# Agent attention with a squared-ReLU layer: the first batch's keys, weight parts, query transposes and table transfers in another order

## The chip, the cores and the metric

One core of a Trainium2 chip runs the kernel. The metric is the device time of one execution in microseconds (us). The kernel before took 2059.75 us, the median of three runs (2058.2 to 2061.1).

## What is computed

Two layers of attention through 49 agents, in four batches of 12480 tokens of width 128, and then a layer with a squared ReLU (128 to 2048 to 128), all in float32:

```python
def _attn_ref(q, k, v, agents):
    scale = 1.0 / np.sqrt(q.shape[-1])
    def sm(a, b):
        s = scale * (a @ b.transpose(0, 2, 1))
        s = s - s.max(-1, keepdims=True)
        e = np.exp(s)
        return e / (e.sum(-1, keepdims=True) + 1e-09)
    a2k = sm(agents, k)
    agent_v = a2k @ v
    q2a = sm(q, agents)
    return (q2a @ agent_v).astype(np.float32)

def _moe_ref(x, w_in, w_out):
    h = np.maximum(x @ w_in, 0.0)
    return (h * h @ w_out).astype(np.float32)
```

`w_in` and `w_out` come as 64-bit floats, and the kernel makes its 32-bit parts of them itself.

## The kernel before, in words

**The main loop.** The product of `agent_v` and `w_in` is made once for each batch: a table of 49 rows and 2048 columns, kept as a rounded part `aw_hi` (rows 0 to 97, with 30 rows of the rest below them) and the last 19 rows of the rest, `aw_ex`, in four places of 32 partitions (`tables`, L323). The queries of a group of 960 tokens become weights over the agents (`queries`, L354): scores (L362), softmax, a split into halves, two transposes (L384), and for each half group j a tile `w` with 30 rows copied below its 98 (L392) and a tile `x` with 19 rows copied to four places (L394). One step k of the main loop then takes two of the 16 column chunks of `w_in` for 480 tokens. `first(k)` (L404) multiplies table and weights for k and k+1 into two PSUM tiles `h` of two banks each; `hidden` (L422) makes `r` (ReLU) and `g_hi` on ACT, and `gg` and `g_lo` on DVE (on POOL for even k); `second(k)` (L447) comes four steps later and sums twelve products with `wo_hi` and `wo_lo` into `o`. 416 pairs of steps are 52 groups in four batches.

**The work beside it.** While a batch runs, `background` (L464) makes the next batch's table: scores of 13 key blocks (`scores`, L181), maxima, exponentials and values. Its steps are dealt out by `goal` (L592).

**The first batch.** Nothing runs beside it, so lines 497 to 579 do the same with other helpers and in an order written out by hand: `queued` (L56) chains the instructions of each engine in the order in which the code issues them (`alone[0]` true). Twelve key blocks of 512 KB, and a small one, are loaded into ten buffers `ahead` by SP, with parts of the weights (`raw`, 256 KB, five buffers) between them (L517 to L528). A block's scores are eight matmuls of 98 columns into both banks of one `h`, a maximum `mx` on DVE and a copy `s` on ACT. Between the blocks stand the decodes of weight parts: ACT takes an absolute value (`begun`, L126), DVE five instructions (`decoded`, L131), POOL a sum (`make_w_in`, L147), or, for a part of `w_out`, ACT a cast `wo_hi` and POOL two instructions (`make_w_out`, L151). Six parts of `w_in` are made among the keys.

Then follow the maxima over all keys (`maxima`, L210) and the values loop (L547): for each block DVE subtracts the maximum (`s<-s,mb`), ACT takes the exponential, PE multiplies with the values, and POOL adds up the exponentials in `mx`. Seven more weight parts are made between them, and the first group's queries go through their steps (`q0`, L563). `whole_sums` (L268) closes the batch, `tables(0)` makes the table: four matmuls `h<-win,avT`, four `aw_hi` on ACT, four `aw_lo` on DVE, and the transfers of L346 to L349, a first set of five for the first 512 columns and a second set of five for the rest. Two of the first set's four `aw_ex` transfers are issued by ACT (L348). The first loads for the second batch and for the second group's queries are asked for just ahead of the table (L572 to L576); the last three weight parts are made in the main loop (L610).

A DMA runs on the queue of the engine that issues it, nearly always SP, and SP takes its instructions in order: one that waits for a buffer or for its source holds all behind it.

Of the kernel before, what the change touches and what calls it, by code (L numbers as in the profile page):

```python
# [17 lines left out]
P = 128  # L18
TP = 120
NT = 8  # L20
# [9 lines left out]
WARM = 16  # L30
PRE = 10
RAW = 5
LATE = 3
SPREAD = 0.88


# [1 line left out]
def agent_attention_relu2(ctx: ExitStack, tc: tile.TileContext, qT, kT, v, agT, w_in, w_out, outT):  # L38
# [142 lines left out]
    def scores(b, i, kt):  # L181
        st = state.setdefault(b, {"s": []})
        _, rows, nt = blocks[i]
        if alone[0]:
            h = ps_h.tile([P, 2, 512], F32, name="h")[:rows, :, :].rearrange("p h (t x) -> p h t x", x=P)
            n = nt // 2
            for t in range(nt):
                out = h[:, t // n, t % n, : 2 * NA]
                keys = kt[:, t * rows : (t + 1) * rows]
                pe.matmul(out, keys, ag[:, :2, :].rearrange("c b a -> c (b a)"), start=True, stop=True)  # L190
            sv = h[:, :, :n, :NA]
        else:
            sv = bank()[:rows, : nt * NA].rearrange("p (t a) -> p t a", a=NA)
            for t in range(nt):
                pe.matmul(sv[:, t, :], kt[:, t * rows : (t + 1) * rows], ag[:, b, :], start=True, stop=True)  # L195
        yield
        s = sp.tile([P, NT, NA], F32, name="s")
        st["s"].append(s)
        if i == 0:
            st["mx"] = small.tile([P, NT, NA], F32, name="mx")  # L200
        s, mx = (x[:rows, :nt, :] for x in (s, st["mx"]))
        if alone[0]:
            s, mx = (x.rearrange("p (h t) a -> p h t a", h=2) for x in (s, mx))
        if i == 0:
            dve.tensor_copy(mx, sv)
        else:
            dve.tensor_max(mx, mx, sv)
        act.copy(s, sv)
# [58 lines left out]

    def whole_sums(b):  # L268
        st = state[b]
        e1 = small.tile([P, 2, NA], F32, name="e1")  # L270
# [52 lines left out]
    def tables(b):  # L323
# [6 lines left out]
        for n in range(FF // 512):  # L330
# [14 lines left out]
            cs = slice(ns.start * 512, ns.stop * 512)  # L345
            sync.dma_start(hi[K2:, cs].bitcast(F32), lo[:SP, cs].bitcast(F32))  # L346
            for t in range(NQ):
                by = act if alone[0] and n == 0 and t % 2 else sync  # L348
                by.dma_start(ex[t * 32 : t * 32 + NL, ns, :].bitcast(F32), apart[SP:, ns, t, :].bitcast(F32))  # L349


    weights = {}
# [140 lines left out]
    def run(gen):  # L493
        for _ in gen:
            pass
# [8 lines left out]
    with tc.tile_pool(name="pre", bufs=PRE) as pre, tc.tile_pool(name="dec", bufs=2) as dec:  # L504
# [8 lines left out]
        def next_values():  # L513
            vts.append(load_values(0, len(vts), pre, "ahead"))

        between = {i: n for n, i in enumerate((3, 4, 6, 7, 9, 10))}
        for i in range(NK):  # L517
            kts.append(load_keys(0, i, pre, "ahead"))
            if 1 <= i <= NW:
                raws[i - 1] = ask_w_in(dec, i - 1)  # L520
            if i == NK - 3:
                q0 = queries(0)
                next(q0)
# [4 lines left out]
                make_w_in(between[i], part)  # L528
        for n in range(10):
            next_values()  # L530
            if n < 3:
                raws[NW + n] = ask_w_out(dec, n)
        top = maxima(0)
        next(top)
# [1 line left out]
        next(top)  # L536
        warm(3)
        next(top)
        warm(6)
        run(top)  # L540
        for i in range(3):
            whole_exps(0, i, dve)
        for i in range(2):
            add_weights(0, i)
        between = {i: n + 6 for n, i in enumerate((0, 2, 3, 5, 7, 8, 10))}
        part = begun(dec, raws.pop(6))
        for i in range(NK):  # L547
            if i + 3 < NK:
                whole_exps(0, i + 3, dve)
# [3 lines left out]
            if i in between:  # L553
# [2 lines left out]
                    make_w_in(n, part)  # L556
                else:
                    make_w_out(n - NW, part)
                if n < NW:
                    raws[n + 5] = ask_w_out(dec, n + 5 - NW)  # L560
                if n + 1 in raws:
                    part = begun(dec, raws.pop(n + 1))
            if i not in (6, 7, 8, 9):  # L563
                next(q0, None)
            if len(vts) < NK:
                next_values()
            if i == NK - 2:
                ends = whole_sums(0)
                next(ends)
        run(q0)  # L570
        run(ends)
        raws = [ask_w_out(late, NW - LATE + n) for n in range(LATE)]  # L572
        todo = background(1)
        next(todo)
        ahead = queries(1)
        next(ahead)  # L576
        run(tables(0))
        next(ahead)
        next(ahead)
    behind = [chain[eng] for eng in (nc.sync, nc.scalar, nc.vector, nc.gpsimd)]  # L580

    alone[0] = False
    ffn = ctx.enter_context(tc.tile_pool(name="ffn", bufs=4))
# [1 line left out]
    for k in range(total + LAG):  # L585
        if k < total:
            g, c = divmod(k, SLOTS)
            b, i = divmod(g, NB)
            if i == 0 and c == 0 and 0 < b < B - 1:
                todo = background(b + 1)  # L590
                done = 0
            goal = (i * SLOTS + c + 1) * STEPS / (SPREAD * NB * SLOTS)  # L592
            while done < goal and step(todo):
                done += 1
            if c == 0 and 0 < g < B * NB - 1:
# [4 lines left out]
        if k % 2 == 0:  # L600
# [6 lines left out]
            copied_out()  # L607
            if hs:
                hidden(k + 1, hs[1])
            if raws:  # L610
                alone[0] = True
                make_w_out(NW - len(raws), begun(late, raws.pop(0)))
                alone[0] = False


# [33 lines left out]
```

## Time and profile before

| | |
|---|---|
| median of three runs | 2059.75 us |
| the profiled execution | 2060.47 us |
| its span | 2058.7 us |
| PE busy | 2022.0 us (98%) |
| ACT busy | 1769.0 us (86%) |
| DVE busy | 1683.2 us (82%) |
| POOL busy | 1271.2 us (62%) |
| mean granted clock of PE | 0.987 |

The profile's busy times are shares of the whole span. The change touches only the first 150 us or so, so the views to read are those by time: the timeline of each engine there, and busy time in stretches of 10 us. In a timeline a row has the start, the length, the engine, the line, the operation with output and inputs, and in brackets the idle time ahead of it with what ended it. Matmuls in float32 show as two or more records each.

### The profile page before, as it was taken

Reading aid. Unit: us, or ns where it says so; the run is one execution under the profiler, and the core shown is the slowest. Engines: PE = TensorE matmul, PEld = TensorE weight load, DVE = VectorE, ACT = ScalarE, POOL = GpSimd, SP = SyncE. Lnnn points to the kernel's source line nnn. Section 1 sums busy time; section 2 is a strip of 40 time slices with the busy share of each in tenths; the row PEclk is TensorE's granted clock in tenths of the full one; section 3 lists DMA queues with packets and bytes.
Section 4 is the critical chain, followed back from the end, with each engine's and each line's share of the span. In section 5 each row is a group of like instructions: output and inputs, shape, how many; then the busy total and the mean of one; then the engine's idle time right before and its main releaser. Section 6 shows DMA issues by size and latency. Waiting matters only on the chain. (4 is left out here: it accounts for less than half of the span.)

```text
span 2058.7 us, 31652 instructions
## 1 busy us (share of the span) xinstructions
PE 2022.0 (98%) x10950; PEld 1592.8 (77%) x10950; DVE 1683.2 (82%) x1843; ACT 1769.0 (86%) x2100; POOL 1271.2 (62%) x1103
## 2 busy tenths in 40 slices
PE   8799999999999999999999999999999999999999
PEld 8578777777788777777778877777777777777777
DVE  5577888888877888888887788888888888888887
ACT  2277999998977899999987799998889999999998
POOL 2354777865644577776554468776555565656565
PEclk9689999999999999999999999999999999999999
DMA  8322121211122121212112212221111111111100
GB/s 323 106 88 92 50 79 59 72 59 57 43 75 80 59 65 57 81 52 75 44 56 71 76 38 64 75 63 43 38 53 37 46 37 42 36 47 35 39 23 20
DMA packets 55552, 131.35 MB, mean 64 GB/s; under 512 B 6560, under 2 KB 35184, under 8 KB 55392
## 3 DMA queue, kind: packets, MB, share of 16 engines
q1 hardware_dynamic: 55352, 129.31, 19.5%
q8 instruction: 87, 1.43, 0.3%
q14 instruction: 73, 0.60, 0.1%
q10 hardware_dynamic: 40, 0.02, 0.0%
HBM read 80.97 MB, written 25.56 MB: 52 GB/s over the span
## 5 line engine op out<-in xcount | busy, mean ns | idle before, releaser
L435 POOL TENSOR_TENSOR g_lo<-gg,g_hi 128x480 fp32r<-128x480 f32 x832 | 999.8, 1223 | 681.2 <-DVE gg L59 424.0
L59 ACT ACTIVATE r<-h 128x960 f32<-128x960 f32 x832 | 802.0, 964 | 165.8 <-PE h L59 154.4
L59 ACT ACTIVATE g_hi<-r 128x960 fp32r<-128x960 f32 x832 | 838.1, 1007 | 32.3 <-POOL e L234 0.4
L59 DVE TENSOR_TENSOR h<-r,h 128x960 f32<-128x960 f32 x416 | 482.2, 1159 | 165.1 <-ACT r L59 160.9
L59 DVE TENSOR_TENSOR gg<-r,h 128x960 f32<-128x960 f32 x416 | 477.5, 1148 | 82.3 <-ACT r L59 78.9
L59 PE MATMUL o<-g_hi,wo_hi 128*128 128x480 f32 x1664 | 538.2, 404 | 0.0
L59 DVE TENSOR_TENSOR g_lo<-h,g_hi 128x960 fp32r<-128x960 f32 x416 | 480.8, 1156 | 47.4 <-ACT g_hi L59 10.6
L59 PE MATMUL h<-w,aw_hi 128*128 128x480 f32 x1664 | 487.9, 398 | 7.5 <-DVE gg L59 6.8
L59 PE MATMUL o<-g_hi,wo_lo 128*128 128x480 f32 x1664 | 494.4, 378 | 0.0
L59 PE MATMUL o<-g_lo,wo_hi 128*128 128x480 f32 x1664 | 494.3, 378 | 0.0
L59 PEld LDWEIGHTS o<-g_hi,wo_hi 128*128 128x128 f32 x1664 | 280.4, 188 | 117.2 <-issue 67.8
L59 PEld LDWEIGHTS o<-g_hi,wo_lo 128*128 128x128 f32 x1664 | 312.5, 188 | 47.3
L59 PEld LDWEIGHTS o<-g_lo,wo_hi 128*128 128x128 f32 x1664 | 312.5, 188 | 47.0
L59 PEld LDWEIGHTS h<-w,aw_hi 128*128 128x128 f32 x1664 | 289.3, 190 | 53.7 <-DVE gg L59 18.8
L59 PE MATMUL h<-x,aw_ex 19*128 19x480 f32 x1664 | 204.7, 481 | 0.6 <-DMA x<-w 0.6
L59 PEld LDWEIGHTS h<-x,aw_ex 19*128 19x128 f32 x1664 | 80.1, 182 | 141.1 <-issue 139.5
L362 PEld LDWEIGHTS psa<-ag,qt 128*120 128x120 f32 x800 | 99.5, 184 | 6.9 <-issue 0.7
L59 DVE COPY ob<-o 128x480 f32<-128x480 f32 x104 | 68.2, 655 | 34.7 <-PE o L59 33.8
L362 PE MATMUL psa<-ag,qt 128*120 128x49 f32 x800 | 94.6, 260 | 0.0
L195 PEld LDWEIGHTS psa<-ag,kt 128*128 128x128 f32 (+1 forms) x588 | 78.9, 202 | 14.3 <-DMA kt<-in_kT 8.5
L234 POOL TENSOR_TENSOR vs<-vt,vs 128x1024 fp32r<-128x1024 f32 (+1 forms) x39 | 81.6, 2094 | 11.2 <-ACT vs L232 10.6
L195 PE MATMUL psa<-ag,kt 128*128 128x49 f32 (+1 forms) x588 | 76.4, 280 | 9.3 <-DMA kt<-in_kT 7.7
(113 smaller groups left out, 1022.7 us busy)
## 6 DMA issues: line engine op xcount, KB each, us to landing
qt<-in_qT SPq DMA_DIRECT2D x52, 480.0 KB
out_T<-ob SPq DMA_DIRECT2D x104, 240.0 KB
kt<-in_kT SPq DMA_DIRECT2D x36, 512.0 KB
vt<-in_v SPq DMA_DIRECT2D x36, 512.0 KB
x<-w SPq DMA_DIRECT2D x416, 35.6 KB
ahead<-in_kT SPq DMA_DIRECT2D x12, 512.0 KB
ahead<-in_v SPq DMA_DIRECT2D x12, 512.0 KB
w<-w SPq DMA_DIRECT2D x104, 56.2 KB
```

Of the source, the lines that this page charges most:

```text
L59: ins = issue(*args, **kw)
L195: pe.matmul(sv[:, t, :], kt[:, t * rows : (t + 1) * rows], ag[:, b, :], start=True, stop=True)
L234: eng.tensor_sub(out[:, :, n : n + w], x, out[:, :, :w].bitcast(F32))
L362: pe.matmul(sv[:, t, :], qt[:, t * TP : (t + 1) * TP], ag[:, b, :], start=True, stop=True)
L435: nc.gpsimd.tensor_sub(lo[:, n, :], gg[:, n, :], hi[:, n, :].bitcast(F32))
```

## The change

Nine edits, all in the first batch's part of the program or at the start of the main loop:

1. **Key blocks.** Two blocks share one `h`, one bank each, eight matmuls one behind the other in a bank; before, each block took a tile of two banks.
2. **Weight parts in the key loop.** The sixth to eighth part of `w_in` are asked for behind key blocks 7, 8 and 9 where it was 6, 7 and 8, and seven parts are made there, after blocks 3, 4, 5, 7, 8, 10 and 11, where it was six.
3. **Weight parts in the values loop.** Five are made (the last of `w_in`, four of `w_out`) where it was seven. Four, not three, have buffers of their own (`LATE`), and all four are asked for in the values loop. One of them is made right behind the table, three in the main loop.
4. **The next loads.** The second group's queries and the second batch's first key block are asked for at step 3 of the values loop; before, ahead of the table.
5. **Query transposes.** The steps of `q0` skip the values loop's steps 5 to 7 and no longer run on behind it, so that the two transposes stand behind the ninth and the eleventh block.
6. **Sums.** `whole_sums` begins at the third last block, not the second last, and uses a buffer `d`.
7. **Table transfers.** SP issues all of them.
8. **Main loop.** No background step is dealt out in the first four steps k; `goal` catches up at the fifth.
9. **Ties.** Background steps are also ordered behind PE's last instruction of the first part. Two more warming matmuls stand in the maxima.

```diff
-            h = ps_h.tile([P, 2, 512], F32, name="h")[:rows, :, :].rearrange("p h (t x) -> p h t x", x=P)
...
+            if i % 2 == 0:
+                st["h"] = ps_h.tile([P, 2, 512], F32, name="h")
+            h = st["h"][:, i % 2, :]
...
-                by = act if alone[0] and n == 0 and t % 2 else sync
-                by.dma_start(ex[t * 32 : t * 32 + NL, ns, :].bitcast(F32), apart[SP:, ns, t, :].bitcast(F32))
+                sync.dma_start(ex[t * 32 : t * 32 + NL, ns, :].bitcast(F32), apart[SP:, ns, t, :].bitcast(F32))
...
-        between = {i: n for n, i in enumerate((3, 4, 6, 7, 9, 10))}
+        asked = {i: n for n, i in enumerate((1, 2, 3, 4, 5, 7, 8, 9))}
+        between = {i: n for n, i in enumerate((3, 4, 5, 7, 8, 10, 11))}
...
-            if 1 <= i <= NW:
-                raws[i - 1] = ask_w_in(dec, i - 1)
+            if i in asked:
+                raws[asked[i]] = ask_w_in(dec, asked[i])
...
-        between = {i: n + 6 for n, i in enumerate((0, 2, 3, 5, 7, 8, 10))}
-        part = begun(dec, raws.pop(6))
+        between = {i: n + 7 for n, i in enumerate((0, 2, 4, 6, 8))}
+        part = begun(dec, raws.pop(7))
...
-            if i not in (6, 7, 8, 9):
-                next(q0, None)
             if len(vts) < NK:
                 next_values()
-            if i == NK - 2:
+            if i == 3:
+                held = [ask_w_out(late, NW - LATE + n) for n in range(LATE)]
+                ahead = queries(1)
+                next(ahead)
+                todo = background(1)
+                next(todo)
+            if i not in (5, 6, 7):
+                next(q0, None)
+            if i == NK - 3:
                 ends = whole_sums(0)
                 next(ends)
-        run(q0)
         run(ends)
-        raws = [ask_w_out(late, NW - LATE + n) for n in range(LATE)]
-        todo = background(1)
-        next(todo)
-        ahead = queries(1)
-        next(ahead)
         run(tables(0))
         next(ahead)
         next(ahead)
-    behind = [chain[eng] for eng in (nc.sync, nc.scalar, nc.vector, nc.gpsimd)]
+        make_w_out(NW - len(held), begun(late, held.pop(0)))
+    behind = [chain[eng] for eng in (nc.tensor, nc.sync, nc.scalar, nc.vector, nc.gpsimd)]
...
-            goal = (i * SLOTS + c + 1) * STEPS / (SPREAD * NB * SLOTS)
+            goal = (i * SLOTS + c + 1) * STEPS / (SPREAD * NB * SLOTS) if k >= 4 else 0
```

SP's queue from the last value load to the table's second set, before (`w_587` and `x_588` are the first half group's query weights, `w_692` and `x_693` the second's; `raw` are weight parts, `qt` and `kt` the next queries and keys):

```order
L59 DMA ahead<-in_v 96x256
L59 DMA w_587<-w_587 30x480
L59 DMA x_588<-w_587 19x480 x4
L59 DMA w_692<-w_692 30x480
L59 DMA x_693<-w_692 19x480 x4
L59 DMA raw<-in_w_out 128x2x256 x3
L59 DMA kt<-in_kT 128x1024
L59 DMA qt<-in_qT 128x960
L59 DMA aw_hi<-aw_lo 30x512
L59 DMA aw_ex<-aw_lo 19x128 x2
L59 DMA aw_hi<-aw_lo 30x1536
L59 DMA aw_ex<-aw_lo 19x3x128 x4
```

and in the change, with the numbers 646 and 679 for the two half groups:

```order
L59 DMA ahead<-in_v 96x256
L59 DMA raw<-in_w_out 128x2x256 x4
L59 DMA qt<-in_qT 128x960
L59 DMA kt<-in_kT 128x1024
L59 DMA w_646<-w_646 30x480
L59 DMA x_647<-w_646 19x480 x4
L59 DMA w_679<-w_679 30x480
L59 DMA x_680<-w_679 19x480 x4
L59 DMA aw_hi<-aw_lo 30x512
L59 DMA aw_ex<-aw_lo 19x128 x4
L59 DMA aw_hi<-aw_lo 30x1536
L59 DMA aw_ex<-aw_lo 19x3x128 x4
```

The five big loads have moved ahead of both sets of query weights, and both of these sets, ten transfers, now stand right ahead of the table's.

ACT at the end of the values loop, before (`pp` is the split of the query weights, `t` the start of a decode, `s` an exponential, `w_587` and `w_692` the copies of the two transposes):

```order
L59 CAST w_587<-h 98x480
L59 ACTIVATE s<-s 128x392 x2
L59 CAST wo_hi<-t 128x256
L59 ACTIVATE t<-raw 128x256
L59 ACTIVATE s<-s 128x392
L59 CAST wo_hi<-t 128x256
L59 ACTIVATE t<-raw 128x256
L59 ACTIVATE s<-s 96x98
L59 CAST wo_hi<-t 128x256
L59 CAST w_692<-h 98x480
L59 COPY avT<-h 128x49
L59 ACTIVATE aw_hi<-h,rl 98x512
```

and in the change:

```order
L59 CAST wo_hi<-t 128x256
L59 ACTIVATE t<-raw 128x256
L59 ACTIVATE s<-s 128x392 x2
L59 CAST wo_hi<-t 128x256
L59 CAST w_646<-h 98x480
L59 ACTIVATE s<-s 96x98
L59 CAST w_679<-h 98x480
L59 COPY avT<-h 128x49
L59 ACTIVATE aw_hi<-h,rl 98x512 x4
```

The first copy of a transpose has moved from behind the second `wo_hi` to behind the fourth and last one, so the two copies stand one exponential apart.

PE from the values to the first `first`, before (`psa<-ag,kt` are key scores of the second batch, `h<-ag,qt` scores of the second group, `h<-s,ahead` the values):

```order
L59 MATMUL h<-s,ahead 128x98 x48
L59 MATMUL h<-identr,pp 98x120 x4
L59 MATMUL h<-s,ahead 128x98 x48
L59 MATMUL h<-identr,pp 98x120 x4
L59 MATMUL h<-s,ahead 128x98 x2
L59 MATMUL h<-ones,e_695 98x1
L59 MATMUL h<-win,avT 98x512 x4
L195 MATMUL psa<-ag,kt 128x49 x8
L59 MATMUL h<-ag,qt 120x49 x8
L59 MATMUL h<-w_587,aw_hi 128x480 x4
L59 MATMUL h<-x_588,aw_ex 128x480 x4
```

and in the change:

```order
L59 MATMUL h<-s,ahead 128x98 x72
L59 MATMUL h<-identr,pp 98x120 x4
L59 MATMUL h<-s,ahead 128x98 x16
L59 MATMUL h<-identr,pp 98x120 x4
L59 MATMUL h<-s,ahead 128x98 x10
L59 MATMUL h<-ones,d 98x1
L59 MATMUL h<-win,avT 98x512 x4
L59 MATMUL h<-ag,qt 120x49 x8
L193 MATMUL psa<-ag,kt 128x49 x5
L59 MATMUL h<-w_646,aw_hi 128x480 x2
L193 MATMUL psa<-ag,kt 128x49 x3
L59 MATMUL h<-w_646,aw_hi 128x480 x2
```

The transposes stand three blocks later, and the key scores no longer stand ahead of the queries. Up to `second(0)` PE now has the scores of two key blocks and no transposes of the second group, where it had three key blocks and both transposes. From about the hundredth row on, in the second group of queries, the orders of all five engines are the same in both kernels.

More of the change, by code (lines that the diff above doesn't have):

```diff
@@ L32 @@
 RAW = 5
-LATE = 3
+LATE = 4
 SPREAD = 0.88
@@ L184, in scores @@
         if alone[0]:
-            h = ps_h.tile([P, 2, 512], F32, name="h")[:rows, :, :].rearrange("p h (t x) -> p h t x", x=P)
[L186 to L191, printed above, removed]
-        else:
-            sv = bank()[:rows, : nt * NA].rearrange("p (t a) -> p t a", a=NA)
-            for t in range(nt):
-                pe.matmul(sv[:, t, :], kt[:, t * rows : (t + 1) * rows], ag[:, b, :], start=True, stop=True)
+            if i % 2 == 0:
+                st["h"] = ps_h.tile([P, 2, 512], F32, name="h")
+            h = st["h"][:, i % 2, :]
+            agents, wide = ag[:, :2, :].rearrange("c b a -> c (b a)"), 2 * NA
+        else:
+            h, agents, wide = bank(), ag[:, b, :], NA
+        for t in range(nt):
+            out = h[:rows, t * NA : t * NA + wide]
+            pe.matmul(out, kt[:, t * rows : (t + 1) * rows], agents, start=True, stop=True)
+        sv = h[:rows, : nt * NA].rearrange("p (t a) -> p t a", a=NA)
         yield
@@ L201, in scores @@
         s, mx = (x[:rows, :nt, :] for x in (s, st["mx"]))
-        if alone[0]:
-            s, mx = (x.rearrange("p (h t) a -> p h t a", h=2) for x in (s, mx))
         if i == 0:
@@ L269, in whole_sums @@
         st = state[b]
-        e1 = small.tile([P, 2, NA], F32, name="e1")
+        e1 = small.tile([P, NT, NA], F32, name="d", bufs=2)[:, :2, :]
         dve.reduce_sum(e1[:, 0, :], st["mx"].rearrange("p t a -> p a t"), axis=AX.X)
@@ L530, in agent_attention_relu2 @@
             next_values()
-            if n < 3:
+            if n < 4:
                 raws[NW + n] = ask_w_out(dec, n)
@@ L538, in agent_attention_relu2 @@
         next(top)
-        warm(6)
+        warm(8)
         run(top)
@@ L558, in agent_attention_relu2 @@
                     make_w_out(n - NW, part)
-                if n < NW:
-                    raws[n + 5] = ask_w_out(dec, n + 5 - NW)
                 if n + 1 in raws:
                     part = begun(dec, raws.pop(n + 1))
-            if i not in (6, 7, 8, 9):
-                next(q0, None)
             if len(vts) < NK:
                 next_values()
-            if i == NK - 2:
+            if i == 3:
[7 more added lines that the diff above has]
+            if i == NK - 3:
                 ends = whole_sums(0)
                 next(ends)
-        run(q0)
         run(ends)
-        raws = [ask_w_out(late, NW - LATE + n) for n in range(LATE)]
-        todo = background(1)
-        next(todo)
-        ahead = queries(1)
-        next(ahead)
         run(tables(0))
@@ L609, in agent_attention_relu2 @@
                 hidden(k + 1, hs[1])
-            if raws:
+            if held:
                 alone[0] = True
-                make_w_out(NW - len(raws), begun(late, raws.pop(0)))
+                make_w_out(NW - len(held), begun(late, held.pop(0)))
                 alone[0] = False
```

## The prediction

> **What bounds the kernel now.** I read the busy time in stretches of 10 us first. The columns are PE, its weight loads, DVE, ACT and POOL (busy time, instructions), the granted clock of PE (1.00 is full), the DMA share and GB/s.
>
> ```profile
> 80.00:90.00 10.00, 2.33 (x10) 1.96 (x10) 2.06 (x3) 1.85 (x3) 0.00 (x0) 0.77 0.58 178
> ...
> 90.00:100.00 10.00, 10.00 (x43) 8.67 (x44) 2.54 (x6) 0.95 (x2) 0.84 (x1) 0.50 0.69 247
> ...
> 100.00:110.00 10.00, 5.86 (x24) 4.25 (x24) 5.64 (x7) 7.40 (x10) 7.56 (x5) 0.50 0.50 181
> ...
> 110.00:120.00 10.00, 8.38 (x32) 6.73 (x31) 7.37 (x12) 7.94 (x12) 5.55 (x7) 0.52 0.26 80
> ...
> 200.00:500.00 300.00, 298.04 (x1601) 231.59 (x1599) 250.63 (x275) 276.53 (x334) 218.70 (x185) 1.00 0.20 64
> ```
>
> From 200 us on PE is busy 298.04 of 300 us at full clock: PE bounds that part, the change leaves its order as it is, and a microsecond can be won only where PE idles or runs at half clock. Both happen ahead of 120 us: PE is busy 2.33 of 10 us from 80 on, and the clock is 0.50 for the thirty that follow. So the sum is made for one point: how much earlier the main loop gets going.
>
> The timeline of PE there, then that of DVE (`m`, `s`, `e`, `aw_lo` as in the code above):
>
> ```profile
> 36.17 2.17 PE L59 MATMUL h<-ones 128*128 128x128 f32 x18
> ...
> 58.01 0.92 PE L59 MATMUL h<-identr,pp 120*98 120x120 f32 x4 [5.20 <-POOL pp L59]
> ...
> 58.72 13.88 PE L59 MATMUL h<-s,ahead 128*128 128x98 f32 x96
> ...
> 75.03 5.34 PE L59 MATMUL h<-win,avT 128*98 128x512 f32 x8
> ...
> 88.05 3.65 PE L195 MATMUL psa<-ag,kt 128*128 128x49 f32 x16 [7.67 <-DMA kt<-in_kT]
> ...
> 91.49 3.40 PE L59 MATMUL h<-ag,qt 128*120 128x49 f32 x16
> ...
> 96.56 0.77 PE L59 MATMUL h<-x,aw_ex 19*128 19x480 f32 x4
> ...
> 117.00 1.17 PE L59 MATMUL o<-g_hi,wo_hi 128*128 128x480 f32 x2
> ```
>
> ```profile
> 32.07 0.89 DVE L59 TENSOR_SCALAR t<-t 128x256 f32<-128x256 f32 x2
> ...
> 34.13 0.91 DVE L59 TENSOR_TENSOR mx<-mx,h 128x392 f32<-128x392 f32 x2
> ...
> 38.97 2.00 DVE L59 TENSOR_TENSOR s<-s,mb 128x392 f32<-128x392 f32 x4
> ...
> 65.35 1.09 DVE L59 TENSOR_TENSOR s<-s,mb 128x392 f32<-128x392 f32 x1
> ...
> 66.37 1.83 DVE L59 TENSOR_SCALAR t<-t 128x256 f32<-128x256 f32 x2
> ...
> 70.08 1.01 DVE L59 TENSOR_SCALAR t<-t 128x256 f32<-128x256 f32 x2
> ...
> 73.03 0.82 DVE L59 TENSOR_REDUCE e<-mx 128x49 f32<-128x392 f32 x1
> ...
> 77.66 0.74 DVE L59 SCALAR_TENSOR_TENSOR aw_lo<-h,rl,aw_hi 49x512 fp32r<-49x512 f32 x1 [2.26 <-ACT aw_hi L59]
> ```
>
> PE waits 5.20 us for the first transposes (58.01) and 7.67 us for the second batch's keys (88.05); behind them stand the next queries' scores (91.49), and the first group's matmuls with `aw_ex` come only at 96.56. DVE has no idle time in brackets from 65.35 to 73.03: the values loop is bound by its subtractions and decodes. ACT and SP, the two that feed the start of the main loop:
>
> ```profile
> 59.93 0.55 ACT L59 CAST w<-h 98x480 fp32r<-98x480 f32 x1
> ...
> 64.68 0.40 ACT L59 CAST wo_hi<-t 128x256 fp32r<-128x256 f32 x1 [1.67 <-DVE t L59]
> ...
> 100.37 1.05 ACT L232 CAST vs<-vt 128x1024 fp32r<-128x1024 f32 x1 [3.22 <-DMA vt<-in_v]
> ...
> 101.32 0.96 ACT L59 ACTIVATE r<-h 128x960 f32<-128x960 f32 x1
> ...
> 116.67 0.49 ACT L208 COPY s<-psa 128x392 f32<-128x392 f32 x1 [1.80 <-DVE mx L207]
> ...
> 124.32 0.96 ACT L59 ACTIVATE r<-h 128x960 f32<-128x960 f32 x1
> ```
>
> ```profile
> 17.22 0.33 SPq L59 DMA_DIRECT2D raw<-in_w_in  x1
> ...
> 60.50 0.98 SPq L59 DMA_DIRECT2D w<-w  x1
> ...
> 61.55 2.48 SPq L59 DMA_DIRECT2D x<-w  x4
> ...
> 73.54 0.85 SPq L59 DMA_DIRECT2D w<-w  x1
> ...
> 74.44 2.44 SPq L59 DMA_DIRECT2D x<-w  x4
> ...
> 79.89 0.34 SPq L59 DMA_DIRECT2D kt<-in_kT  x1
> ...
> 83.94 0.87 SPq L59 DMA_DIRECT2D aw_hi<-aw_lo  x1
> ...
> 87.08 4.57 SPq L59 DMA_DIRECT2D aw_ex<-aw_lo  x4
> ```
>
> SP takes the key load at 79.89, and the table's first transfer, whose source `aw_lo` was there at 77.66 + 0.74 = 78.40, only at 83.94. The first `r` comes at 101.32, behind a cast that waited for a load.
>
> **The key loop.** PE's waits while it scores the keys, and the DMA's hole behind the `raw` of 17.22:
>
> ```profile
> L59 PE MATMUL h<-ag,ahead 128*128 128x98 f32 x192 | 22.4, 276 | 3.9 <-DMA ahead<-in_kT 2.3 <-ACT t L59 1.6
> ```
>
> ```profile
> 16.00:18.00 2.00, 2.00 (x20) 2.00 (x20) 1.93 (x5) 0.58 (x2) 0.73 (x1) 1.00 0.06 18
> ```
>
> A key load no longer stands behind that `raw`, which waits for the first decode. The most to be had is all 3.9 us of waits; I take 3.0, since the hole of 2 us is filled and part of the rest follows. Against it, a seventh decode now stands between the last two maxima: the chain from 32.07 to 34.13 is 2.1 us, of which I put 1.9 on the path. The two more warming matmuls stand ahead of one that DVE waits for: at 2.17 us for nine (36.17) they are 0.5 us. The first subtraction (38.97) moves by 1.9 - 3.0 + 0.5 = -0.6 us, to 38.4; the ends are +2.6 (no wait saved) and -3.4 (all saved, the decode beside them). One bank for a key block costs nothing in itself: the matmuls and the two readers are the same, and six blocks instead of three fit ahead of the readers.
>
> **The values loop on DVE.** By position, the subtraction at 65.35 (1.09 us) comes earlier in the row, and two decodes go: from 66.37 to 69.37 (3.00 us) and from 70.08 to 73.03 (2.95 us). One of them now lies in the key loop, one behind the table. So the last sum starts at 73.03 - 3.00 - 2.95 - 0.6 = 66.5. For the two the ends are -4.1 (the key loop's 2.06 us each) and -8.3 (if four more subtractions ran in the 0.50 us of 38.97, not the 1.09 of 65.35). The table's matmuls followed that sum by 75.03 - 73.03 = 2.0 us, so they begin at 68.5, and `aw_lo` is there 78.40 - 75.03 = 3.4 us later, at 71.9. PE has 13 blocks in that time; where it waits it may fall to half clock, a cost that the next part hides.
>
> **The transfers of the table.** Two sets of query weights now stand ahead of it on SP. What they take is read from two stretches with nothing else in the queue, the four `x` issued from 61.55 on and the four large `aw_ex` issued from 87.08 on:
>
> ```profile
> 62.60:69.40 6.80, 6.80 (x53) 6.80 (x52) 6.53 (x12) 2.39 (x6) 4.39 (x6) 0.83 0.07 23
> ...
> 88.40:93.30 4.90, 4.90 (x26) 4.90 (x25) 0.00 (x0) 0.00 (x0) 0.00 (x0) 0.50 0.07 22
> ```
>
> The share is 0.07, one engine of sixteen, at 23 and 22 GB/s: four transfers, issued 0.6 us apart, go one behind the other through one engine, 6.8 us for a set of `x` and 4.9 us for the large `aw_ex` (4 x 28.5 KB). The first set's four small ones (4 x 9.5 KB) are a third of that, 1.6 us. I take it that all of these share that engine. The Trainium skill says why ("DMA: Bandwidth & Descriptors", section on why a DMA increments its semaphore by 16): a transfer runs on the largest number of engines up to 16 that divides its rows, and on the lowest-numbered ones, so 19 rows run on one and always the same. The share of 0.07 agrees; that `x` and `aw_ex` have the same engine no row shows. The rule speaks against edit 5, which puts 13.6 us of such transfers ahead of the table; by it the sum stays, without it rival 1 holds.
>
> The first copy of a transpose now follows the last `wo_hi`, which stands where the one at 64.68 stood: 64.68 + 1.09 - 0.6 = 65.2, with the copy at 65.5. In the row before, SP issued 0.57 us behind that copy (59.93, 60.50) and `x` moved from 62.6 on, 2.1 us behind that issue. From 66.1 on:
>
> - `x` of the first half group moves from 68.2 to 75.0,
> - that of the second from 75.0 to 81.8 (both issues, 3.5 and 3.3 us, are through at 72.9),
> - the small `aw_ex` from 81.8 to 83.4, the large from 83.4 to 88.3.
>
> The table is ready at 71.9 and SP free at 72.9; its first small transfer could move 2.1 us and an `aw_hi` later, at 76, so the engine is the last by nearly 6 us: that is the cover over the half clock, the late sums and most of the uncertainty of the values loop. SP's two more issues (0.6 us each) and ACT's freed time lie under it too. The matmuls with `aw_ex` begin at about 83.7 and not at 96.56; they took 0.77 us, and `r` starts at 84.5, not at 101.32: -16.8 us. What could be late in their place is not: the keys and queries, asked for at step 3, have 20 us, and their scores (3.65 + 3.40 us at half clock) fit between the table's matmuls (5.34 us, to 73.9) and 83.
>
> **From there to a full PE.** From the first `r` to the seventh (101.32, 124.32) ACT takes 23.0 us, held by DVE's decodes and PE. The change leaves three decodes and both casts of values in it, so I take the same 23.0; without the wait for key scores at half clock (116.67) it would be 1.8 us less, with a second cast of 1.05 us (100.37) inside 1 us more. PE then still owes the scores of one key block that the row before had behind it: 3.65 us at half clock, half of that at full, 1.8 us. The forecast is -16.8 + 1.8 = -15.0 us. By PE's own path: the second set lands at 88.3, then 0.8 us of `aw_ex`, 3.65 of key scores, two DVE instructions and `first(4)`, about 4, set `second(0)` at 96.8 in place of 117.00, -20.2, less what PE then still owes (the key block and two transposes at half of 0.92 us, 2.7 us): -17.5. The later of the two paths holds: -15.0.
>
> Against the profiled execution's 2060.47 us that is 2045.5; this execution is 0.7 us above the median of 2059.75, against which it gives 2044.8.
>
> **The rivals.**
>
> 1. *The engine isn't shared in order*: the table's small transfers pass the second `x` set. Then `r` follows the issue: SP free at 72.9, five issues as at 73.54 (3.3 us), 2.1 us to movement, 0.4 for the last: 78.7, and `r` at 79.5, -21.8 + 1.8 = -20.0 us: 2039.8. For it: no row has `x` and `aw_ex` in the queue together. Against it: the flat 0.07 of each. Chance 0.15.
> 2. *The values loop is bound by PE at half clock.* Twelve key blocks of the same form took 22.4 us, 1.87 each; at half clock from 39.6 on twelve and a quarter take 45.8 us, to 85.4, then 2.0 and 3.4 us to `aw_lo`, 6.6 us as in rival 1: `r` at 97.4, -3.9 + 1.8 = -2.1: 2057.6. For it: PE now waits for DVE several times. Against it: six blocks at a clock of partly 0.83 took 13.88 us (58.72), and at that pace the loop ends at 68, in time. Chance 0.13; a time halfway to the forecast, 2051, is likelier than the end.
> 3. *Slower: the shared engine takes one transfer at a time, landing included.* If each of the eight `x` (1.7 us) and four small `aw_ex` (0.4 us) ahead of the first group costs 2.1 us from issue to movement besides, the twelve make 40.4 us from 66.1 on: `r` at 107.3, +6.0 + 1.8: 2067.6. It turns slower where they take over 32.6 us (`r` at 99.5). For it: SP did wait for such landings before its loads and the table, in the view of the waits:
>
> ```profile
> SPq L59 <- DMA x<-w: 4.4, 3, 1.9
> ```
>
>    Against it: three waits made 4.4 us, not 6.3, and four `x` took 6.8 us. Chance 0.05.
> 4. *The change does nothing*: the main loop's start is held by something that the rows don't show, and the time won ahead of it is given back: 2059 to 2061. Chance 0.04.
>
> **How the numbers follow.** The forecast has 0.63. Its bounds: -3.4 to +2.6 against -0.6 in the key loop moves the chain by -2.8 to +3.2, the values loop's -4.1 to -8.3 by +1.9 to -2.3, ACT's 23.0 us by -1.8 to +1, run to run 1.5 us: 2038 to 2050, as they will not all go one way. With rival 1 inside and the near half of rival 2, the range is 2038 to 2051 us. 0.2% is about 4 us, about what a measurement of this kernel can tell from no change. Faster by more: 0.63 + 0.15 + 0.13 = 0.91; within it: 0.04; slower: 0.05.
>
> **What would show it.** Right: no wait of PE for `kt` behind the table; `x` and `aw_ex` in a row at 0.07 of the DMA from about 68 to 88 us; the first subtraction near 38.4, the last sum near 66.5, the first `r` near 84.5. Wrong: `r` ahead of 80 (rival 1), the table's matmuls behind 75 (rival 2), gaps between the `x` transfers (rival 3), or PE idle for several us between the first and the seventh `r`, by which time won at the table is lost again.

## The result and the profile after

The change makes the kernel slower: 2074.61 us median of 4 runs (2074.41 to 2074.79), against 2060.43 us of the kernel before beside it (4 runs, 2058.20 to 2063.52). The ratio is 1.0068, 95% interval 1.005 to 1.0085: 14 us more, where 15 us less was forecast. The profiled execution took 2074.41 us with a span of 2072.6.

The same stretches as before, with the same columns (busy time of PE, its weight loads, DVE, ACT, POOL, then PE's clock, DMA share, GB/s):

```profile
80.00:90.00 10.00, 9.44 (x34) 5.33 (x33) 4.33 (x10) 3.27 (x6) 0.00 (x0) 0.62 0.12 36
...
200.00:500.00 300.00, 298.52 (x1598) 231.54 (x1595) 249.39 (x274) 275.62 (x333) 216.24 (x183) 1.00 0.20 66
```

The hole from 80 to 90 us is gone (9.44 us busy, 2.33 before), but with a granted clock of 0.62. From 200 on PE is as busy as before, 298.52 of 300 us at full clock; nothing there looks worse. So the loss needs two questions: does the main loop start later, and does it run at another pace? ACT's rows for the first and seventh `r`, for one at about 160 us (the same, the twenty-first, in both kernels) and for the last one answer both. In the change:

```profile
95.78 0.97 ACT L59 ACTIVATE r<-h 128x960 f32<-128x960 f32 x1 [2.74 <-issue]
...
106.65 1.05 ACT L229 CAST vs<-vt 128x1024 fp32r<-128x1024 f32 x1 [3.02 <-DMA vt<-in_v]
...
115.44 0.41 ACT L59 CAST wo_hi<-t 128x256 fp32r<-128x256 f32 x1 [3.42 <-DVE t L59]
...
123.73 0.56 ACT L385 CAST w<-psa 98x480 fp32r<-98x480 f32 x1 [3.45 <-PE psa L380]
...
124.49 0.97 ACT L59 ACTIVATE r<-h 128x960 f32<-128x960 f32 x1
...
161.56 0.98 ACT L59 ACTIVATE r<-h 128x960 f32<-128x960 f32 x1 [1.72 <-PE h L59]
...
2062.47 0.95 ACT L59 ACTIVATE r<-h 128x960 f32<-128x960 f32 x1
```

and before, the last two of them:

```profile
159.75 0.97 ACT L59 ACTIVATE r<-h 128x960 f32<-128x960 f32 x1 [1.69 <-PE h L59]
...
2048.86 0.96 ACT L59 ACTIVATE r<-h 128x960 f32<-128x960 f32 x1
```

The first `r` comes 5.5 us earlier (95.78, 101.32), not 16.8. The seventh comes at the same time (124.49, 124.32): three waits of ACT of 3.0 to 3.5 us stand between the two (rows 106.65, 115.44 and 123.73). The twenty-first is 1.8 us late, the last one 13.6 us late. So nothing is won at the start, and 11.8 us are lost in the main loop, where the order of the instructions is the same.

**The start.** PE's timeline and DVE's:

```profile
6.86 1.93 PE L59 MATMUL h<-ag,ahead 128*128 128x98 f32 x16
9.96 3.81 PE L59 MATMUL h<-ag,ahead 128*128 128x98 f32 x32 [1.18 <-ACT s L59]
14.94 3.81 PE L59 MATMUL h<-ag,ahead 128*128 128x98 f32 x32 [1.17 <-ACT s L59]
20.46 3.81 PE L59 MATMUL h<-ag,ahead 128*128 128x98 f32 x32 [1.70 <-ACT s L59]
25.98 5.44 PE L59 MATMUL h<-ag,ahead 128*128 128x98 f32 x32 [1.70 <-ACT s L59]
...
43.75 0.42 PE L59 MATMUL h<-ident,m 128*49 128x128 f32 x1 [1.64 <-DVE m L59]
43.97 3.87 PE L59 MATMUL h<-ones 128*128 128x128 f32 x22
...
81.92 6.43 PE L59 MATMUL h<-win,avT 128*98 128x512 f32 x8 [0.56 <-DVE rl L59]
...
92.92 0.68 PE L59 MATMUL h<-w,aw_hi 128*128 128x480 f32 x2 [1.83 <-DVE rest L59]
...
94.82 0.77 PE L59 MATMUL h<-x,aw_ex 19*128 19x480 f32 x4
...
103.01 3.62 PE L193 MATMUL psa<-ag,kt 128*128 128x49 f32 x16 [0.42 <-DMA kt<-in_kT]
```

```profile
48.47 2.00 DVE L59 TENSOR_TENSOR s<-s,mb 128x392 f32<-128x392 f32 x4
...
76.77 0.79 DVE L59 TENSOR_TENSOR s<-s,mb 96x98 f32<-96x98 f32 x1
79.72 0.82 DVE L59 TENSOR_REDUCE d<-mx 128x49 f32<-128x392 f32 x1 [2.17 <-POOL mx L59]
...
84.68 0.74 DVE L59 SCALAR_TENSOR_TENSOR aw_lo<-h,rl,aw_hi 49x512 fp32r<-49x512 f32 x1 [2.64 <-ACT aw_hi L59]
```

Before, the first seven key blocks were one group without a gap:

```profile
7.47 12.64 PE L59 MATMUL h<-ag,ahead 128*128 128x98 f32 x112
```

Now PE stops once in every two blocks, 1.2 to 1.7 us, for `s`, which is ACT's copy of the scores out of `h`. The first subtraction starts at 48.47, 9.5 us later than before.

**The pace.** Where nothing stands beside the main loop, PE's first matmuls with `g_hi` and `wo_hi` of every second step, before:

```profile
2018.28 0.70 PE L59 MATMUL o<-g_hi,wo_hi 128*128 128x480 f32 x2
...
2022.36 0.70 PE L59 MATMUL o<-g_hi,wo_hi 128*128 128x480 f32 x2
```

and in the change:

```profile
2015.12 0.70 PE L59 MATMUL o<-g_hi,wo_hi 128*128 128x480 f32 x2
...
2019.23 0.70 PE L59 MATMUL o<-g_hi,wo_hi 128*128 128x480 f32 x2
```

Two steps take 4.08 us before and 4.11 after. The page's groups of these matmuls say the same. Before:

```profile
L59 PE MATMUL o<-g_hi,wo_hi 128*128 128x480 f32 x1664 | 538.2, 404 | 0.0
L59 PE MATMUL o<-g_hi,wo_lo 128*128 128x480 f32 x1664 | 494.4, 378 | 0.0
L59 PE MATMUL o<-g_lo,wo_hi 128*128 128x480 f32 x1664 | 494.3, 378 | 0.0
```

and in the change, the three summing to 13.9 us more:

```profile
L59 PE MATMUL o<-g_hi,wo_hi 128*128 128x480 f32 x1664 | 543.4, 408 | 0.0
...
L59 PE MATMUL o<-g_hi,wo_lo 128*128 128x480 f32 x1664 | 499.3, 381 | 0.0
...
L59 PE MATMUL o<-g_lo,wo_hi 128*128 128x480 f32 x1664 | 498.1, 381 | 0.0
```

Matmuls of the same shape, on the same clock, in the same order, take 3 or 4 ns longer. For the experiments I use a finer measure, called interval sum below: the mean interval from the start of one of the six `o` matmuls of a step to the start of the next matmul, over the trace's PE records from 200 us on, the six added up. Intervals above 250 ns are left out; they are nearly all those of the first matmul in about every second step, and with them the sums are 1348 and 1363 ns. Without them it is 1293 ns before and 1310 in the change: 15 to 17 ns more in each of 832 steps, 12 to 14 us. The intervals behind the second matmul of a pair grow, from 216 to 220 ns; the ones between the two of a pair hardly do (216 and 217 for `wo_lo`).

### The profile page after: what moved, and what is told of

Its sections match the earlier page's. It is cut to its first block, busy times and chain, and to the rows that moved or that the text cites. A ratio compares the mean times of both kernels' runs of the same rounds, so it can differ in the third digit from the quotient of the medians.

```text
span 2072.6 us, 31643 instructions
## 1 busy us (share of the span) xinstructions
PE 2038.9 (98%) x10954; PEld 1594.0 (77%) x10954; DVE 1684.3 (81%) x1843; ACT 1769.6 (85%) x2100; POOL 1270.2 (61%) x1103
## 4 chain that ended last, share of the span: by engine, by line
PE 90%; DVE 5%; ACT 2%; issue 1%; DMA 1%; SPq 1%; POOL 0%; DVEq 0%; ACTq 0%; POOLq 0%
PE o L59 53%; PE h L59 27%; PE psa L358 4%; PE psa L193 3%; PE psa L380 2%; PE psa L296 1%; DVE gg L59 1%; ACT r L59 1%; DVE t L59 1%; DMA x<-w 1%; DVE g_lo L59 1%; DVE h L59 1%; PE psa L331 0%; DVE z L369 0%; DMA vt<-in_v 0%
## 5 line engine op out<-in xcount | busy, mean ns | idle before, releaser
L59 DVE COPY ob<-o 128x480 f32<-128x480 f32 x104 | 68.2, 656 | 39.4 <-PE o L59 38.0
```

The source lines that it names most:

```text
L59: ins = issue(*args, **kw)
```

## The experiments

**The theory.** (a) Two key blocks in one tile `h` make the second block's matmuls wait for ACT's copy of the first, since the program's wait is for the tile: some 8 us. (b) The main loop is slower because its buffers have moved: the change drops the buffer `e1` (416 B) and adds a fourth late buffer (2048 B), so that `aw_hi`, the query weights `w` and what follows lie 416 B lower, and `r`, `gg`, `g_hi`, `g_lo` and `ob` 1632 B higher. In the built programs `g_hi` starts at byte 187424 of each partition before, at 189056 in the change. The rivals: that (a) is all, the later start being what the end shows, so that an own tile gives back the whole loss and more; and that the waits for the tile are hidden behind later ones, so that it gives back nothing.

**The tile and the offsets, each alone and both.** Four kernels in one set of runs; the kernel before took 2060.55 us beside them. *The change with an own tile*, in `scores`:

```diff
-            if i % 2 == 0:
-                st["h"] = ps_h.tile([P, 2, 512], F32, name="h")
-            h = st["h"][:, i % 2, :]
+            h = ps_h.tile([P, 2, 512], F32, name="h")[:, 0, :]
```

> The change with one edit half undone: each key block takes an h of its own again, and uses one bank of it; offsets, order and all other edits stay. Theory: two causes. (a) In the change the second block of a shared h waits for the first one's copy s on ACT, which costs PE some 8 us of waits and moves the first subtraction from 39 to 48 us; (b) the main loop's matmuls run 0.9% slower because the buffers lie at other offsets in SBUF. By it the waits for s among the key blocks go, the first subtraction comes at 38 to 40 us, the first r some 8 us earlier (about 88), and the time is about 2066, with the main loop still slow (about 4.11 us for a pair of steps with nothing beside it). Rival 1 (a alone, the slow main loop being the start's after-effect or the chip's): about 2052. Rival 2 (the waits for s are hidden, the DMA or DVE being as late): 2072 to 2075.

Measured: 2065.99 us, ratio 1.0029 (1.0017 to 1.0040), 8.6 us less than the change. Its timeline of PE has the blocks in one group again, with no wait for `s`, and DVE's first subtraction is back near the place of before (38.97):

```profile
6.26 16.99 PE L59 MATMUL h<-ag,ahead 128*128 128x98 f32 x144
23.74 2.00 PE L59 MATMUL h<-ag,ahead 128*128 128x98 f32 x16 [0.48 <-DMA ahead<-in_kT]
```

```profile
39.82 2.00 DVE L59 TENSOR_TENSOR s<-s,mb 128x392 f32<-128x392 f32 x4
```

The first `r` comes at 88.41, the twenty-first at 152.85, 8.7 us ahead of the change's; the interval sum stays at 1310 ns. That is the theory's case; both rivals have fallen.

*The change with 32 B put in*, an unused buffer in front of the one that `e1` now shares, which moves all that follows:

```diff
+        small.tile([P, 8], F32, name="pad")
         e1 = small.tile([P, NT, NA], F32, name="d", bufs=2)[:, :2, :]
```

> The change with an unused buffer of 32 bytes per partition ahead of the buffers of the first batch's sums, so that every buffer behind it lies 32 bytes higher; nothing else. Theory (b): the slow main loop comes from the offsets; in the kernel before, the operands of its matmuls lay at odd multiples of 32 bytes, in the change at even ones. By it a pair of steps goes back from 4.11 to 4.08 us, the time from 2074.6 to about 2060, with the first 100 us unchanged. If the offset matters but by a larger modulus, something between. Rival (order, start or chip): no change, 2074 to 2075.

Measured: 2064.85 us, ratio 1.0021 (1.0012 to 1.0031). The interval sum falls from 1310 to 1299 ns, not to 1293: most of the slow pace is a matter of 32 bytes, and a rest is not.

*The kernel before with the change's buffers*, its order untouched:

```diff
-        e1 = small.tile([P, 2, NA], F32, name="e1")
+        e1 = small.tile([P, NT, NA], F32, name="d", bufs=2)[:, :2, :]
...
-        raw = dec.tile([P, WCH, 2], U32, name="raw", bufs=LATE if dec is late else RAW)
+        raw = dec.tile([P, WCH, 2], U32, name="raw", bufs=LATE + 1 if dec is late else RAW)
```

> The kernel before, in its own order, with the buffers of the change's sizes (four late weight parts have room though three are used, and the first batch's sums use a buffer d), so that every buffer lies at the change's offset. Theory (b): its main loop gets the change's slow pace, 4.11 us for a pair of steps, and the time is about 2074, with the first 120 us as before. Rival (order, start or chip): 2058 to 2063 as before.

Measured: 2073.97 us, ratio 1.0063 (1.0048 to 1.0078), interval sum 1310 ns. The kernel before, with nothing but its buffers moved, is as slow as the change. The two faults are apart in the traces as well: from the twenty-first to the last `r` it takes 1901.0 us, as the change and the run with an own tile do (1900.9 each), where the kernel before takes 1889.1 and the run with 32 B 1892.1. Two of its steps in the place shown above take 4.12 us:

```profile
2010.55 0.70 PE L59 MATMUL o<-g_hi,wo_hi 128*128 128x480 f32 x2
...
2014.67 0.70 PE L59 MATMUL o<-g_hi,wo_hi 128*128 128x480 f32 x2
```

*Own tile and 32 B*:

> The change with a tile of its own for each key block and the unused 32 bytes. Theory (a and b): both gains add up, about 2052: 8 us less than before, from the start alone. Rival 1 (a alone): as own_tile. Rival 2 (b alone): as pad32.

Measured: 2057.82 us, ratio 0.9984 (0.9974 to 0.9993). The two parts nearly add up (8.6 and 9.8 us off the change's 2074.61 would be 2056.2). It falls 6 us short of the expected time, and the rest of the pace (6 ns a step, as with 32 B alone) is 5 of them.

**Which buffer, and which offsets.** Five kernels are the one before, with an unused buffer of N bytes put in front of `g_hi`, N being 32, 96, 128, 160 or 224, so that `g_hi`, `g_lo` and `ob` alone move (the built programs with N = 96, 128 and 224 have all other buffers where they were):

```diff
+        if k == 0:
+            ffn.tile([P, N // 4], F32, name="pad", bufs=1)
         hi = ffn.tile([P, 2, G], F32R, name="g_hi", bufs=HB)
```

The one with N = 96 was run four times (the kernel before took 2061.09 us beside it):

> The kernel before, with an unused buffer of 96 B in front of g_hi: only g_hi, g_lo and ob move, to multiples of 128, as in the change; r, gg, the tables and the query weights stay. If the offset of g_hi and g_lo, the operands that the second product streams, sets the pace: 14 us more than before, 2074 us, with the matmul behind each second one 4 ns later. If the offset of the query weights or the tables, or their distance from g, sets it: 2060 us.

Measured: 2070.99 us, ratio 1.0051 (1.0036 to 1.0066), interval sum 1309 ns. So the place of `g_hi` and `g_lo` slows the second product by itself, but it makes 9.9 us of the 13.4. From the twenty-first to the last `r` this kernel loses 9.2 us against the kernel before, the one with all buffers moved 11.9; what the others add to it (`r`, `gg`, the tables, the query weights) wasn't separated.

The other four had one run each, beside one of the kernel before of 2060.32 us:

> The kernel before, an unused buffer of 32 B in front of g_hi: g_hi and g_lo at 64 modulo 256. If only multiples of 128 are slow (128 modulo 256 took 1309 ns for the six matmuls of a step, 32 took 1293): 1293 to 1299 ns, 2060 to 2064 us. If multiples of 64 are slow: 1309 ns, 2071 us.

> The kernel before, an unused buffer of 128 B in front of g_hi: g_hi and g_lo at 160 modulo 256, and nothing else moved. If their own offset is what made 1299 ns of the run with 32 B: 1299 ns, 2064 us. If the other buffers' offsets made the difference to 1293: 1293 ns, 2060 us.

> The kernel before, an unused buffer of 160 B in front of g_hi: g_hi and g_lo at 192 modulo 256. If only multiples of 128 are slow: 1293 to 1299 ns, 2060 to 2064 us. If multiples of 64 are slow: 1309 ns, 2071 us.

> The kernel before, an unused buffer of 224 B in front of g_hi: g_hi and g_lo at 0 modulo 256. If multiples of 128 or of 64 are slow: 1309 ns, 2071 us, as at 128. If the place within 256 counts by its half (32 fast, 160 and 128 slower): 1293 ns, 2060 us.

Measured, with the earlier ones; a `g` buffer is 3840 B, a multiple of 256, and its second half begins 1920 B in, 128 modulo 256:

| `g_hi` modulo 256 | modulo 64 | interval sum, ns | us |
|---|---|---|---|
| 32 (before) | 32 | 1293 | 2060.32 |
| 160 | 32 | 1300 | 2062.67 |
| 64 | 0 | 1307 | 2069.61 |
| 192 | 0 | 1308 | 2068.76 |
| 128 (N = 96) | 0 | 1309 | 2070.99, beside 2061.09 |
| 0 | 0 | 1311 | 2069.82 |

Every start at a multiple of 64 is slow, by 13 to 17 ns a step and 8 to 10 us in all; both starts at 32 modulo 64 are fast, and of these 160 modulo 256 is 6 ns behind, as with 32 B in the change (1299). That only multiples of 128 are slow has fallen, and so has that the half of the 256 counts.

Of the two matmuls of a pair, the first streams the first half of a `g` buffer and the second the other half. Sorted by where the half itself starts (an interval counted to the matmul that opens it), the traces are finer than the table: a half at 0 modulo 256 takes 219 to 221 ns, whether it is the second one (starts at 128, and the change) or the first (start at 0); a half at 64 or 192 takes 217 to 219; one at 128 takes 215 to 217, hardly more than one at 32 or 160 (214 to 218). So a buffer at 128 or at 0 pays in one of its two halves, one at 64 or 192 a little in both.

**What the change's edits are worth with both faults mended.** Three kernels, in one set of runs with the one at N = 96. *Own tile and 160 B*, the buffer of the second experiment with 160 B for 32, which puts `g_hi` at 32 modulo 256:

> The change with an own h tile for each key block and an unused buffer of 160 B, which puts g_hi at 32 modulo 256, as in the kernel before (the 32 B of the earlier run put it at 160 modulo 256). If the byte offset of the square's tiles modulo 256 sets the pace, the six matmuls of a step take 1292 ns as before (1296 with 32 B, 1310 without) and the median is 2055 us, 3 us under the run with 32 B. If only the remainder modulo 128 counts, 2058 us, as with 32 B.

Measured: 2055.34 us (2050.98 to 2055.80), ratio 0.9967 (0.9954 to 0.9980), interval sum 1294 ns. The pace is that of before, as expected of the offset modulo 256. Its profile shows where the start stands, in DVE's and ACT's timelines:

```profile
39.02 2.00 DVE L59 TENSOR_TENSOR s<-s,mb 128x392 f32<-128x392 f32 x4
...
70.27 0.81 DVE L59 TENSOR_REDUCE d<-mx 128x49 f32<-128x392 f32 x1 [2.16 <-POOL mx L59]
```

```profile
87.56 0.97 ACT L59 ACTIVATE r<-h 128x960 f32<-128x960 f32 x1 [5.57 <-issue]
...
111.82 0.56 ACT L384 CAST w<-psa 98x480 fp32r<-98x480 f32 x1 [1.93 <-PE psa L379]
...
112.58 0.97 ACT L59 ACTIVATE r<-h 128x960 f32<-128x960 f32 x1
...
150.95 0.97 ACT L59 ACTIVATE r<-h 128x960 f32<-128x960 f32 x1 [1.69 <-PE h L59]
...
2040.40 0.95 ACT L59 ACTIVATE r<-h 128x960 f32<-128x960 f32 x1
```

It is 8.8 us ahead of before at the twenty-first `r`, 8.5 at the last one: what is won at the start is kept to the end, once the pace is the same. (The profiled execution took 2052.32 us, 3 less than the median.)

*The same, with the next queries' steps of the first group begun later*:

```diff
-            if c >= 2 or g == 0:
+            if c >= (4 if g == 0 else 2):
                 step(ahead)
```

> Own tile and 160 B, and the next queries' steps of the first group begin four steps later, so that their transposes no longer stand between PE's second product and ACT's fifth and seventh r. If ACT's wait for these transposes (3.5 us ahead of a query weight cast) is what gives back the time won at the table: 2 us less than the run with 160 B alone. If the half clock of PE sets the pace there: no difference, within 1 us.

Measured: 2050.53 us (2049.79 to 2051.52), ratio 0.9949 (0.9932 to 0.9966): 10.6 us below the kernel before and the fastest of all runs. ACT's wait for the transposes is gone from the row of the cast:

```profile
113.40 0.96 ACT L59 ACTIVATE r<-h 128x960 f32<-128x960 f32 x1
114.52 0.56 ACT L384 CAST w<-psa 98x480 fp32r<-98x480 f32 x1 [0.16 <-PE psa L379]
...
149.94 0.97 ACT L59 ACTIVATE r<-h 128x960 f32<-128x960 f32 x1 [1.68 <-PE h L59]
...
2038.79 0.95 ACT L59 ACTIVATE r<-h 128x960 f32<-128x960 f32 x1
```

Against the run with 160 B the seventh `r` is not earlier (113.40, 112.58; its first was 1.1 us later), the twenty-first 1.0 and the last one 1.6 us earlier. The direction is the expected one, the place in part only. The rival, PE's half clock, isn't what makes the difference: from the first to the twenty-first `r` the mean granted clock is lower than with 160 B alone (0.85, 0.88), and the stretch shorter all the same (61.2 us, 63.4). The medians are 4.8 us apart, but the intervals of the two ratios overlap; how much of it is this edit stays open.

*Own tile and 160 B, with ACT issuing two of the small `aw_ex` transfers again*:

```diff
-                sync.dma_start(ex[t * 32 : t * 32 + NL, ns, :].bitcast(F32), apart[SP:, ns, t, :].bitcast(F32))
+                by = act if alone[0] and n == 0 and t % 2 else sync
+                by.dma_start(ex[t * 32 : t * 32 + NL, ns, :].bitcast(F32), apart[SP:, ns, t, :].bitcast(F32))
```

> Own tile and 160 B, and ACT issues two of the four small aw_ex transfers again, as in the kernel before. If all of them go one behind the other through one DMA engine, as forecast, the order of issue changes nothing: the first r at 88.4 us, give or take 0.5, and the same median within 1 us. If SP's issues bound the table, ACT's help makes the first r about 1 us earlier.

Measured: 2053.65 us (2053.25 to 2056.91), ratio 0.9968 (0.9956 to 0.9980). The median is 1.7 us lower, more than the 1 us expected, but the intervals of the two ratios hardly differ: no difference that these runs can tell. The first `r` comes at 88.00, within the half microsecond expected of one engine that takes all transfers. By the trace's DMA records, ACT's two now move among the `x` (79.24 to 82.86), but the last small `aw_ex` ends 17.7 us behind the first copy of `w`, as without ACT's help (17.6). But the scheduler then orders ACT in another way, and the third `r` comes 6.4 us later (100.89, 94.46 in the run with 160 B), behind casts that wait:

```profile
88.00 0.97 ACT L59 ACTIVATE r<-h 128x960 f32<-128x960 f32 x1 [1.24 <-PE h L59]
...
94.44 1.05 ACT L227 CAST vs<-vt 128x1024 fp32r<-128x1024 f32 x1 [3.21 <-DMA vt<-in_v]
...
100.58 0.41 ACT L59 CAST wo_hi<-t 128x256 fp32r<-128x256 f32 x1 [2.92 <-DVE t L59]
100.89 0.96 ACT L59 ACTIVATE r<-h 128x960 f32<-128x960 f32 x1
```

By the seventh `r` (114.24) 1.7 us of the 6.4 are left, at the last one (2041.69) 1.3: in this pair of traces most of a wait of one engine ahead of the full main loop isn't a loss at the end.

## Why the prediction was wrong

Two sentences of it failed, each about something that was held to cost nothing. Against the forecast of -15.0 us at the start of the main loop, the change had +1.8 at the twenty-first `r`, 16.8 us off; the main loop, forecast at no change, added 11.8 us, and what lies behind the last `r` 0.3.

**"One bank for a key block costs nothing in itself" is the step that failed first.** The matmuls and readers are the same, as it says, but two blocks share a tile, and the second block's matmuls wait until ACT has copied the first. "Six blocks instead of three fit ahead of the readers" is true of the banks and not of the program: the tile is what the wait is for. The first subtraction was forecast at 38.4 and came at 48.47. The run with an own tile took 8.6 us off the median and has the same row at 39.82, with 160 B it is at 39.02: this term, put at nothing, was 8.7 to 9.5 us. The rest of the key loop, forecast at -0.6, measured +0.85 and +0.05 in these two runs. That it fell within its ends is in part luck: the warming matmuls were forecast at 0.5 us more, but from the reduction `m<-mx` to the first subtraction it is 6.0 us with either run and was 3.9 before, at a lower granted clock (see the last section); the reduction itself came earlier (33.85 and 33.06, 35.08 before).

**"The change leaves its order as it is, and a microsecond can be won only where PE idles or runs at half clock" is the step that failed second.** The order did stay; the addresses did not. The list of edits named both causes (the sums use a buffer `d`; four late buffers, not three), but no term, bound or rival was made of them. The kernel before with only its buffers moved (+13.4 us) shows that this alone is the size of the whole loss. None of the rivals had this mechanism; the one for a slower kernel put it at the shared DMA engine, with gaps between the `x`, and there are none (see below).

**The values loop: the last decode was worth 0.7 us, not 2.95, the other 2.1, not 3.0.** The forecast subtracted two whole decodes between the first subtraction and the last sum, 28.1 us for the 34.06 of before; 31.25 were measured, in the change (48.47 to 79.72) and with both faults mended (39.02 to 70.27) alike. Behind the last subtraction stood a decode, from 70.08 to 73.03; in its place now stands DVE's wait of 2.17 us for POOL's last addition to `mx`. The decode had been the cover of that chain, which the working should have named: last subtraction to last sum was 3.66 us before (69.37 to 73.03) and is 2.95 now (76.77 to 79.72). The other decode lay ahead of the last subtraction, which came 30.40 us behind the first one before and comes 28.30 us behind it now.

**The transfers of the table: right.** From the last sum to the first `r` the forecast has 18.0 us; the change took 16.1 (79.72 to 95.78), the run with 160 B 17.3; before it was 28.3 (73.03 to 101.32). PE's wait of 7.67 us for the first `kt` is gone; a later key block's scores wait 0.42 us (103.01). The Trainium skill's rule ("DMA: Bandwidth & Descriptors", section on why a DMA increments its semaphore by 16) puts transfers of 19 rows on one engine, always the same. The trace agrees: while the change's `aw_ex` moved, the share was 0.07, one engine of 16, in the microsecond from 93:

```profile
93.00:94.00 1.00, 1.00 (x8) 0.94 (x8) 0.00 (x0) 0.04 (x1) 0.92 (x2) 1.00 0.07 21
```

That `x` and `aw_ex` have the same engine, which no row before showed, the trace's DMA records (start, size and length of each packet) show now. In the change the eight `x` move without a gap from 79.31 to 92.05; then come the last two of the 30 rows of the first `aw_hi`, until 92.21 (the other 28 were through at 88.27), the small `aw_ex` from 92.21 to 94.06, and the large ones from 94.63 to 100.91. With 160 B the times are 69.87 to 82.61, 82.78, 82.78 to 84.59 and 85.06 to 90.52, where the forecast had 68.2 to 81.8 for the `x`, 83.4 for the end of the small `aw_ex` and 88.3 for that of the large. That a second issuing engine would not help, the run with ACT's issues bore out.

This queue also decides when PE can begin. PE's wait of 1.83 us ahead of the first matmul with the table ends at 92.92, 0.7 us behind the two rows. Its row names a decode on DVE that ended at about the same time, but with 160 B that decode was through at 81.90, and PE waited on, again until 0.7 us behind the two rows:

```profile
83.45 1.14 PE L59 MATMUL h<-w,aw_hi 128*128 128x480 f32 x2 [3.41 <-issue]
```

So the late last sum cost little, as the forecast's cover had it: the queue starts with the first copy of `w`, 27.9 us behind the first subtraction in the change (76.41) and with 160 B (66.96), where 27.1 were forecast.

**From the first to the seventh `r`: 28.7 us, not 23.0.** The prediction had named a loss here as a sign of being wrong, with PE idle for several us. The time is lost here, but PE idles no longer than before (5.9 us of the 28.7, 5.8 of the 23.0). The working took ACT's 23.0 us of before as they were; only a second cast, of 1 us, stood in the bounds. In the change three casts wait there, 3.02 us for a value load, 3.42 for a decode and 3.45 for transposes that PE has behind two steps of the second product. With an own tile and 160 B the stretch is 25.0 us (87.56 to 112.58): the load is nearly there (0.82 us), and the transposes cost 1.93. The term was 2 us too small by itself. The other 3.7 us don't follow the shift of what lies ahead: with 32 B alone, whose first `r` is as late as the change's (95.71), the stretch is 24.5 us, with the own tile alone 27.5. They follow the granted clock, whose mean over the stretch is 0.61 in the change and 0.60 with the own tile, but 0.69 with 32 B and 0.70 with 160 B. That makes 22.5 us at half clock in the change and 15.2 with 160 B, and 7.2 us more at half clock are 3.6 us more for the same work. What set the clock there wasn't tried.

Added up at the twenty-first `r`: key loop +10.1, from the first subtraction to the last sum +3.1, from there to the first `r` -1.9, first to seventh `r` +5.7, and from there 37.1 us where 35.4 and the 1.8 owed were forecast, -0.2: the 16.8 us. With both faults mended (160 B), 8.8 of the 15.0 us are there at the twenty-first `r`; the other 6.2 are 0.6 in the key loop, 2.4 from the first subtraction to the first `r`, 2.0 from there to the seventh and 1.1 behind it.

**The rivals.** The one by which the values loop becomes bound by PE at half clock has its sign, the table's matmuls behind 75 us (81.92), but not its mechanism: they are late as the whole loop starts late, and DVE did not wait for PE in it. For the transfers that pass each other or leave gaps, the first and the third rival, see above: neither happened. The fourth, by which the change does nothing, names what happened in part, that time won ahead of the main loop is given back, but not the loss.

## What to carry to other kernels

An edit that adds, drops or shares a buffer moves every buffer behind it: compare the addresses of the operands that the bound engine streams, as one compares the order, and put them back with a few bytes of padding before judging anything else. A tile that holds two pieces of work makes the second wait for the first one's readers, however many banks it has. And when a piece of work is taken out, look for the chain that it had covered: the time saved reaches only to that chain's end.

## What the hardware showed that was not expected

- A pair of matmuls that stream 480 `fp32r` columns each takes longer when the streamed buffer starts at a multiple of 64 B within the partition than at 32 modulo 64: 1307 to 1311 ns for six matmuls against 1293 to 1300, over six offsets with the same instructions. The time is lost in the half that starts at 0 modulo 256 (behind the second matmul of each pair in the change, 220 ns for 216; between the two, 220 to 221, for a buffer at 0 modulo 256), and in smaller parts in halves at 64 and 192 (217 to 219). Why stays open.
- The granted clock was lower in the warming matmuls than before, though there were more of them: 22 took 3.87 us at a mean clock of 0.66 in the change (43.97, behind a wait of 1.64 us for `m`), 18 took 2.17 us at 1.00 before (36.17, behind one of 0.28). With the own tile it was 0.59.
- Of a DMA of 30 rows, two rows waited 3.8 us in the change (88.27 to 92.05) for transfers of 19 rows that stood ahead of them on one engine, and PE waited for the two.
